# Two-batch MoE after clustered attention: order of the layers, and weights that are converted once and kept in DRAM

## Chip, cores and metric

One NeuronCore of one Trainium2 chip runs the whole program. The metric is the device time of one execution in microseconds (us); the median of three runs is given, and the profile is one profiled execution.

## What is computed

The reference runs three stages one after the other on 2 x 768 tokens:

```python
attn = softmax(where(q_assign == k_assign, q @ k.T / 8, -1e9)) @ v   # 2 batches, 8 heads, 768 x 64
x = attn as [1536, 512]                                              # 768 rows per batch
x = ((x @ w1) * (x @ w2)) @ w3 @ w_out                               # 512 -> 1024 -> 1024 -> 512
h = x @ w_in                                                         # 512 -> 2048
out = (max(h, 0) + alpha * min(h, 0)) @ w_out2                       # 2048 -> 512
```

Here q_assign and k_assign are the nearest of 16 centroids by cosine. The weights arrive as float64 and are read as pairs of 32-bit words.

## The kernel before

Every product of the MoE is made of three matmuls of split operands (mm3, L188 to L191): a float32 operand is held as a pair, hi and lo, and the product is hi x hi, hi x lo and lo x hi. On TensorE all of it is 128 x 128 weight loads, each with 384 or 512 columns streamed past.

The attention runs first, as 96 units (16 heads over both batches, 6 query tiles each), written out as a software pipeline in one loop. In the gaps of that loop (fill_steps, L606) stand the masks of later heads and, once batch 0's heads are done, the first layer of batch 0.

The MoE after it is the loop `for b in range(B)` at L731. w3 and w_out are folded into one matrix wc = w3 @ w_out, so the layers are:

- L1 (l1, L525): for each of 8 blocks f and each half a of the 768 rows, 12 matmuls for x @ w1, 12 for x @ w2, and the product of the two in PR. p_split (L725) then makes the pair ph, pl of PR: a ScalarE cast and a VectorE subtract per half.
- LC (lc, L495): the fold, 8 blocks of 24 matmuls with 512 columns. It is done once, in batch 0, after L1. Its result is kept in SBUF and also stored to DRAM (wcd) for batch 1.
- L2: x2 = PR @ wc, 4 blocks e x 2 halves x 24 matmuls, drained into the pair X2.
- L3 and L4 (l3, L777; l4, L798): 16 blocks f. l3 makes 2 x 12 matmuls with 384 columns, drained through the leaky ReLU (two ScalarE activations at L790 and L791, a VectorE combine at L792, a ScalarE cast at L795, a VectorE subtract at L796) into the pair g. l4 makes 6 x 3 matmuls with 512 columns that accumulate over all f in three PSUM tiles acc. The loop runs l3(f), then l4(f-1).

The order on TensorE is therefore L1(0), LC, L2(0), L3/L4(0), L1(1), L2(1), L3/L4(1). x_split (L509), which makes the pair of the attention's output, stands for batch 1 inside L3/L4 of batch 0.

The weights come as a stream of halves of 512 columns, in the order of the list `halves` (L69 to L80). SyncE loads a raw half (512 KB, L115), ScalarE scales its high words (w_u, L127), VectorE puts float32 words together in three instructions (w_conv, L139, L140, L143), ScalarE casts hi (L170), and GpSimd subtracts lo (L175). w_step (L157) takes the stream one half further: it emits the conversion of half n and the split of half n-1. w_goal emits a step if the stream is behind a given half, w_ready emits steps until a half is there. Both are called by hand between the matmuls, so the order on every engine is that of the code. Batch 1 loads and converts w1, w2, w_in and w_out2 a second time, and it loads wc back from DRAM. In all 120 halves are converted. There are 3 raw buffers, 4 of hi and 4 of lo, and after the attention the layers other than L4 drain through two PSUM banks (alloc_c, L722).

## Time and profile before

| | |
|---|---|
| median of 3 runs | 853.52 us (846.9, 853.52, 854.06) |
| span of the profiled execution, first to last instruction | 852.6 us |
| TensorE busy | 779.9 us, 91% |
| VectorE busy | 666.0 us, 78% |
| ScalarE busy | 508.8 us, 60% |
| GpSimd busy | 395.7 us, 46% |
| moved by DMA | 101 MB, mean 119 GB/s |

No time of the profiled execution other than its span is given; the median lies 0.9 us above the span, and that difference is carried for what lies around the span. The engines work beside each other, each in its own order. The matmuls are pipelined: the time one is shown for (0.33 us) is longer than the distance to the next start, so TensorE's pace is read from starts. Line numbers in rows of the trace are those of the kernel before.

### The profile page before, as it was taken

The page shows a single profiled execution, that of the slowest core. Times are in us where ns is not written, and L with a number is a line of the kernel's source. Part 1 is how long each engine was busy: PE and PEld are TensorE (multiplying, and loading weights), DVE is VectorE, ACT ScalarE, POOL GpSimd, SP SyncE. Part 2 cuts the span into 40 slices and gives each one's busy share as a digit, 9 for nine tenths or more (in the row PEclk, how much of TensorE's full clock was granted, in tenths as well). Part 3 has the DMA queues.
Part 4 walks back from the last instruction along what each step waited for, and adds up shares of the span by engine and source line. Part 5 has one row for each costly group of instructions (what it writes and reads, how often), then busy time and mean ns, then how long its engine had stood idle before and what let it go on. Part 6 is the DMA issues. An engine that isn't in the chain of part 4 may idle for free.

```text
span 852.6 us, 13016 instructions
## 1 busy us (share of the span) xinstructions
PE 779.9 (91%) x4497; PEld 705.1 (83%) x4497; DVE 666.0 (78%) x1020; ACT 508.8 (60%) x1092; POOL 395.7 (46%) x350
## 2 busy tenths in 40 slices
PE   5889899689999999698999989999899999999997
PEld 2778888679999989686799877888799999888886
DVE  2876899988888899969728888888666338888885
ACT  5689898777777695436434555555354335555553
POOL 0576688768485765434433343333233333333331
PEclk9799999889999999899999999999999999999999
DMA  8464333524343303536313322333432133333321
GB/s 257 146 177 142 90 94 93 145 65 117 107 126 100 107 26 125 185 124 210 117 47 108 122 101 100 123 124 122 175 124 104 49 122 122 123 107 117 124 99 75
DMA packets 35890, 101.08 MB, mean 119 GB/s; under 512 B 4496, under 2 KB 8720, under 8 KB 35824
## 3 DMA queue, kind: packets, MB, share of 16 engines
q1 hardware_dynamic: 35824, 100.25, 37.0%
q8 instruction: 36, 0.59, 0.3%
q14 instruction: 30, 0.25, 0.1%
HBM read 80.93 MB, written 5.24 MB: 101 GB/s over the span
## 4 chain that ended last, share of the span: by engine, by line
DVE 34%; PE 30%; issue 13%; ACT 8%; POOL 4%; DMA 1%; SPq 0%; POOLq 0%; DVEq 0%; ACTq 0%
DVE wt L140 13%; DVE wt L139 5%; DVE gr L792 4%; DVE wt L143 4%; ACT g L795 3%; POOL wl L175 3%; PE l L191 3%; DVE pl L465 3%; PE t L455 3%; PE l L190 3%; PE l L189 3%; PE l1b L189 2%; PE l1b L190 2%; PE l1b L191 2%; PE l1a L189 2%
## 5 line engine op out<-in xcount | busy, mean ns | idle before, releaser
L175 POOL TENSOR_TENSOR wl<-wt,wh 128x512 fp32r<-128x512 f32 x112 | 162.2, 1448 | 287.1 <-DVE g L796 171.1
L140 DVE SCALAR_TENSOR_TENSOR wt<-wr,wt 128x512 uint32<-128x512 uint32 x120 | 154.1, 1284 | 4.1
L465 DVE TENSOR_TENSOR pl<-t,ph 128x384 fp32r<-128x384 f32 x192 | 97.7, 549 | 30.7 <-ACT ph L464 30.3
L795 ACT CAST g<-gr 128x384 fp32r<-128x384 f32 x64 | 32.8, 513 | 128.5 <-DVE gr L792 128.5
L455 PE MATMUL t<-cst,p 128*128 128x128 f32 x576 | 86.6, 288 | 22.8 <-DVE pl L465 22.8
L143 DVE SCALAR_TENSOR_TENSOR wt<-wu,wt 128x512 uint32<-128x512 uint32 x120 | 102.1, 851 | 4.1
L464 ACT CAST ph<-t 128x384 fp32r<-128x384 f32 x192 | 83.5, 483 | 33.4 <-PE t L455 31.7
L191 PE MATMUL l<-x2h,wl 128*128 128x384 f32 x256 | 88.7, 347 | 11.4 <-POOL wl L175 11.4
L440 POOL TENSOR_SCALAR p<-p,su 128x768 f32<-128x768 f32 x96 | 88.3, 925 | 16.9 <-DVE su L437 14.5
L422 DVE TENSOR_REDUCE nm<-s 128x1 f32<-128x768 f32 x96 | 91.0, 947 | 4.5 <-PE s L415 4.5
L455 PEld LDWEIGHTS t<-cst,p 128*128 128x128 f32 x576 | 66.3, 146 | 32.7 <-issue 24.9
L429 ACT ACTIVATE p<-s,nm 128x768 f32<-128x768 f32 x96 | 88.0, 917 | 2.8 <-DVE nm L422 2.8
L189 PE MATMUL l<-x2h,wh 128*128 128x384 f32 x256 | 86.1, 336 | 2.2 <-ACT wh L170 2.2
L127 ACT ACTIVATE wu<-wr 128x512 f32<-128x512 f32 x120 | 81.0, 676 | 10.4 <-DMA wr<-in_w3t_dram 7.8
L190 PE MATMUL l<-x2l,wh 128*128 128x384 f32 x256 | 85.8, 335 | 0.0
L170 ACT CAST wh<-wt 128x512 fp32r<-128x512 f32 x112 | 69.3, 619 | 20.9 <-DVE wt L143 20.7
L414 PE MATMUL s<-st 128*128 128x384 f32 x192 | 76.8, 400 | 3.1 <-ACT p L429 3.1
L189 PE MATMUL acc<-wh,g 128*128 128x512 f32 x192 | 75.5, 393 | 3.5 <-ACT g L795 1.6
L476 PE MATMUL o<-ph,vs 128*128 128x256 f32 x288 | 76.8, 293 | 0.0
L191 PE MATMUL acc<-wh,g 128*128 128x512 f32 x192 | 75.9, 395 | 0.0
L190 PE MATMUL acc<-wl,g 128*128 128x512 f32 x192 | 75.7, 394 | 0.0
L477 PE MATMUL o<-pl,vs 128*128 128x256 f32 x288 | 74.9, 287 | 0.0
(132 smaller groups left out, 1907.8 us busy)
## 6 DMA issues: line engine op xcount, KB each, us to landing
wr<-in_w_dram SPq DMA_DIRECT2D x96, 512.0 KB, 3.6
wr<-in_w3t_dram SPq DMA_DIRECT2D x16, 512.0 KB, 4.3
jm<-in_qka_dram SPq DMA_DIRECT2D x12, 512.0 KB, 5.7
hr<-in_qkh_dram SPq DMA_DIRECT2D x16, 384.0 KB, 3.3
st<-st SPq DMA_DIRECT2D x16, 384.0 KB, 3.7
st<-st SPq DMA_DIRECT2D x32, 192.0 KB, 2.7
wr<-in_wo_dram SPq DMA_DIRECT2D x8, 512.0 KB, 3.2
vr<-in_vv_dram SPq DMA_DIRECT2D x8, 384.0 KB, 3.2
```

The lines of the kernel that those rows point to most:

```text
L140: nc.vector.scalar_tensor_tensor(out=t, in0=r[:, :, 0], scalar=29, in1=t, op0=ALU.logical_shift_right, op1=ALU.bitwise_or)
L143: nc.vector.scalar_tensor_tensor(out=t, in0=u, scalar=3, in1=t, op0=ALU.logical_shift_left, op1=ALU.bitwise_or)
L175: nc.gpsimd.tensor_tensor(out=lo, in0=tts.pop(n - 1), in1=f32(hi), op=ALU.subtract)
L189: nc.tensor.matmul(o, lhsT=whi, rhs=xhi, start=first, stop=False)
L190: nc.tensor.matmul(o, lhsT=whi, rhs=xlo, start=False, stop=False)
L191: nc.tensor.matmul(o, lhsT=wlo, rhs=xhi, start=False, stop=last)
L422: nc.vector.tensor_reduce(out=m, in_=scp[i][:, :, 0:HS], op=ALU.max, axis=AX.XY, negate=True)
L429: nc.scalar.activation(out=p.rearrange("p (a k) -> p a k", a=2), in_=scp.pop(i)[:, :, 0:HS], func=AF.Exp, bias=nmax.pop(i), scale=1.0, acc ...
L440: nc.gpsimd.tensor_scalar(out=pt[i], in0=pt[i], scalar1=sums[i // 2][:, i % 2 : i % 2 + 1], scalar2=1.0, op0=ALU.mult, op1=ALU.mult)
L455: nc.tensor.transpose(t[:, k], pt[i][:, kt * P : kt * P + P], ident)
L464: nc.scalar.copy(out=pth[g][:, 3 * a : 3 * a + 3, q], in_=t)
L465: nc.vector.tensor_tensor(out=ptl[g][:, 3 * a : 3 * a + 3, q], in0=t, in1=f32(pth[g][:, 3 * a : 3 * a + 3, q]), op=ALU.subtract)
```

## The change

The list of halves becomes a list `seq` with two kinds of entries. A "c" entry is a raw half that is loaded, converted and split, as before. A "k" entry loads a finished pair hi | lo (512 KB) from a DRAM tensor `kept`. Each half of w1, w2 (key "l1"), w_in and w_out2 (key "w45", second index 0 or 1) is converted once, in batch 0, and its pair is stored to `kept` from SyncE two conversions later; batch 1 has only "k" entries. The w_out2 halves of the first 10 blocks f are converted ahead of L3/L4 (key "e", stored only) and loaded back for batch 0. There are 72 conversions in place of 120, 48 stores and 58 loads of pairs. w_step is cut in two: one call emits the conversion, the next the cast and the subtract of the same half, and w_goal is called about twice as often; the loads of pairs take no call of their own. Pairs share 5 buffers of hi | lo. w_room hands on the oldest of them only when its matmuls, and its store, stand in the program. There are 4 raw buffers and 2 of converted words, in place of 3 and 3.

The order on TensorE becomes L1(0), LC block 0, then L1(1) block f and LC block f+1 in turn, then L2(0), L2(1), L3/L4(0), L3/L4(1), the last two as one loop of 33 turns. wc stays in SBUF as a pair and is split once, from PSUM, by ScalarE and VectorE. p_split of batch 0 moves in front of LC, p_split of batch 1 into L2, and x_split of batch 1 into LC's block 0. Until L3 starts, the layers drain through a ring of five PSUM tiles.

```diff
-    wcd = dp.tile([4, P, 8, P], F32, name="wcd")
-    halves = []
-    l1h = [("w", w12[f, :, k * 512 : k * 512 + 512]) for f in range(8) for k in range(2)]
-    halves += l1h[0:12] + [("wo", g) for g in range(6)] + l1h[12:16] + [("wo", g) for g in range(6, 8)]
...
+    NE = 10
+    kept = dp.tile([48, P, 2, 512], F32, name="kept")
+    seq, at, keep, need = [], {}, {}, {}
...
+    def conv(what, f, k, early=False):
+        key = (what, 0, f, k)
+        stored = what in ("l1", "w45")
+        if stored:
+            keep[what, f, k] = len(keep)
+        item("c", key, w_src(what, f, k), int(stored) + int(not early))
+    def back(what, b, f, k):
+        item("k", (what, b, f, k), keep[what, f, k], 1)
+    for f in range(6):
+        conv("l1", f, 0), conv("l1", f, 1)
+    for g in range(6):
+        conv("wo", g, 0)
+    for f in range(6, 8):
+        conv("l1", f, 0), conv("l1", f, 1)
+    for g in range(6, 8):
...
     for f in range(8):
-        halves += [("w", w3t[f, :, 0:512]), ("w", w3t[f, :, 512:1024])]
...
+        conv("w3", f, 0), conv("w3", f, 1)
+        back("l1", 1, f, 0), back("l1", 1, f, 1)
+    for f in range(NE):
+        conv("w45", f, 1, early=True)
+        at.pop(("w45", 0, f, 1))
+        need["e", f] = need.pop(("w45", 0, f, 1))
+        seq[-1] = ("c", ("e", f), seq[-1][2])
+    for f in range(16):
+        conv("w45", f, 0)
+        if f < NE:
+            back("w45", 0, f, 1)
+        else:
+            conv("w45", f, 1)
+    for f in range(16):
+        back("w45", 1, f, 0), back("w45", 1, f, 1)
+    NSEQ = len(seq)
...
+    def w_store():
+        n = stores.popleft()
+        key = seq[n][1]
+        nc.sync.dma_start(out=kept[kept_at(key)], in_=f32(whole.pop(n)))
+        w_done(key)
+    def w_room():
+        if len(held) < NWHL:
+            return True
+        while stores and need[held[0]] > 0 and seq[stores[0]][1] == held[0]:
+            w_store()
+        return need[held[0]] == 0
...
+        t = wp.tile([P, 2, 512], F32R, tag="whl", bufs=NWHL, name=f"wh{n}")
+        his[key] = t[:, 0], t[:, 1]
...
+    def w_step(force=False):
...
+        kind, key, src = seq[n]
+        if kind == "k":
+            if not w_room():
+                assert not force, key
+                return False
+            nc.sync.dma_start(out=f32(whl_tile(n)), in_=kept[src])
+            st["step"] += 1
+            return True
+        m = ordinal[n]
+        if not st["half"]:
+            w_load(m + 3)
+            while stores and ordinal[stores[0]] <= m - 2:
+                w_store()
+            w_u(m)
+            w_conv(n)
+            w_u(m + 1)
+            st["half"] = 1
+            return True
...
+        else:
+            if not w_room():
+                assert not force, key
+                return False
+            t = whl_tile(n)
+            hi, lo = his[key]
+            if key[0] in ("l1", "w45", "e"):
+                whole[n] = t
+                stores.append(n)
+        nc.scalar.copy(out=hi, in_=tts[n])
+        nc.gpsimd.tensor_tensor(out=lo, in0=tts.pop(n), in1=f32(hi), op=ALU.subtract)
+        st["half"] = 0
...
+        nc.scalar.copy(out=WO["wc"][:, 0, f], in_=t)
+        nc.vector.tensor_tensor(out=WO["wc"][:, 1, f], in0=t, in1=f32(WO["wc"][:, 0, f]), op=ALU.subtract)
...
+        def l1_steps(b, f, ahead):
+            for a in range(2):
+                if a == 0:
+                    w_ready(("l1", b, f, 1))
+                for _ in l1(b, f, a, alloc_f):
+                    w_goal(ahead)
+                    yield f
...
+        ring = deque(("c", "acc0", "c", "acc1", "acc2"))
...
+            nc.scalar.copy(out=ph, in_=PR[b][:, f, s])
+            nc.vector.tensor_tensor(out=pl, in0=PR[b][:, f, s], in1=f32(ph), op=ALU.subtract)
...
+        for f in fill:
+            w_goal(at["w3", 0, 0, 1])
+            w_goal(at["w3", 0, 0, 1])
+            if f is not None and nsp < f:
+                p_split(0, nsp, 0), p_split(0, nsp, 1)
+                nsp += 1
+        w_ready(("w3", 0, 0, 1))
+        while nsp < 8:
+            p_split(0, nsp, 0), p_split(0, nsp, 1)
+            nsp += 1
+        lc(0, alloc_c, lambda k: x_split(1, k))
+        for f in range(8):
+            nxt = min(f + 1, 7)
+            for _ in l1_steps(1, f, at["l1", 1, nxt, 1]):
+                pass
+            if f < 7:
+                w_ready(("w3", 0, f + 1, 1))
+                lc(f + 1, alloc_c, lambda k: w_goal(at["w3", 0, min(f + 2, 7), 1]))
+        X2 = {0: [st_tile(f"x2{t}").rearrange("p e s -> p e s") for t in "hl"]}
+        x = cp.tile([P, 8 * S], F32, tag="wox", name="x2_1").bitcast(F32R).rearrange("p (t e s) -> p t e s", t=2, e=4)
+        X2[1] = [x[:, 0], x[:, 1]]
+        for b, a in ((0, 0), (0, 1), (1, 0), (1, 1)):
+            s = slice(a * HS, a * HS + HS)
+            for e in range(4):
+                t = alloc_c(f"l2_{b}{e}{a}")
+                for f in range(8):
+                    if f % 4 == 0:
+                        w_goal(NSEQ)
+                    c = slice(e * P, e * P + P)
+                    wc = WO["wc"]
+                    mm3(t[:, 0:HS], wc[:, 0, f, c], wc[:, 1, f, c], PH[b, a][:, f], PL[b, a][:, f], f == 0, f == 7)
+                nc.scalar.copy(out=X2[b][0][:, e, s], in_=t[:, 0:HS])
+                nc.vector.tensor_tensor(
+                    out=X2[b][1][:, e, s], in0=t[:, 0:HS], in1=f32(X2[b][0][:, e, s]), op=ALU.subtract
+                )
+                if (b, a) == (0, 1):
+                    p_split(1, 2 * e, 0), p_split(1, 2 * e + 1, 0)
+                if (b, a) == (1, 0):
+                    p_split(1, 2 * e, 1), p_split(1, 2 * e + 1, 1)
...
+        def l3(b, f):
+            w_ready(("w45", b, f, 0))
+            hi, lo = his["w45", b, f, 0]
+            g = big(("ph0", "pl0")[f % 2], f"g{b}{f}")[:, 0 : 2 * S].bitcast(F32R).rearrange("p (t s) -> p t s", t=2)
+            w = big(("ph1", "pl1")[f % 2], f"gr{b}{f}")[:, 0 : 4 * HS].rearrange("p (a t s) -> p a t s", a=2, t=2)
+            G[b, f] = g
...
+                w_goal(NSEQ)
...
+            w_done(("w45", b, f, 0))
...
-            for f in range(17):
-                if f < 16:
-                    w_ready(n_l34(b, f))
-                    l3(f)
...
+        for i in range(33):
+            if i < 32:
+                l3(*divmod(i, 16))
+            if i > 0:
+                l4(*divmod(i - 1, 16))
```

The order of VectorE where the attention is over and the first LC block comes near (wt = words of a converted half, pr = product of L1, pl = lo part that p_split makes), before:

```order
L139 TENSOR_SCALAR wt25_4551<-wu25_4523 128x512
L140 SCALAR_TENSOR_TENSOR wt25_4551<-wr25_4505,wt25_4551 128x512
L143 SCALAR_TENSOR_TENSOR wt25_4551<-wu25_4523,wt25_4551 128x512
L139 TENSOR_SCALAR wt26_4578<-wu26_4549 128x512
L140 SCALAR_TENSOR_TENSOR wt26_4578<-wr26_4530,wt26_4578 128x512
L143 SCALAR_TENSOR_TENSOR wt26_4578<-wu26_4549,wt26_4578 128x512
L537 TENSOR_TENSOR pr0_506<-l1b070_4585,asb070_4571 128x384
```

and now:

```order
L180 SCALAR_TENSOR_TENSOR wt24_4557<-wr24_4462,wt24_4557 128x512
L183 SCALAR_TENSOR_TENSOR wt24_4557<-wu24_4533,wt24_4557 128x512
L798 TENSOR_TENSOR pl00_4472<-pr0_506,ph00_4471 128x384
L798 TENSOR_TENSOR pl01_4476<-pr0_506,ph01_4475 128x384
L179 TENSOR_SCALAR wt25_4587<-wu25_4561 128x512
L180 SCALAR_TENSOR_TENSOR wt25_4587<-wr25_4496,wt25_4587 128x512
L183 SCALAR_TENSOR_TENSOR wt25_4587<-wu25_4561,wt25_4587 128x512
```

Halves 24 and 25 are those of w3's first block, which LC block 0 reads. Before, conversions followed each other; now a pair of pl stands between them, four such pairs ahead of half 25's last instruction.

VectorE in block 4 of L3/L4 of batch 0 (gr = leaky ReLU before its split, g = its pair), before:

```order
L792 SCALAR_TENSOR_TENSOR gr040_5659<-gn040_5660,alp_71,gr040_5659 128x384
L796 TENSOR_TENSOR g04_5633<-gr040_5659,g04_5633 128x384
L139 TENSOR_SCALAR wt59_5671<-wu59_5637 128x512
L140 SCALAR_TENSOR_TENSOR wt59_5671<-wr59_5589,wt59_5671 128x512
L143 SCALAR_TENSOR_TENSOR wt59_5671<-wu59_5637,wt59_5671 128x512
L792 SCALAR_TENSOR_TENSOR gr041_5691<-gn041_5692,alp_71,gr041_5691 128x384
L796 TENSOR_TENSOR g04_5633<-gr041_5691,g04_5633 128x384
L516 TENSOR_TENSOR xs1_5523<-xr6_3489,xs1_5523 128x384
L139 TENSOR_SCALAR wt60_5726<-wu60_5669 128x512
```

and now:

```order
L183 SCALAR_TENSOR_TENSOR wt78_6444<-wu78_6378,wt78_6444 128x512
L865 SCALAR_TENSOR_TENSOR gr04_6417<-gr04_6417,alp_71 128x384
L869 TENSOR_TENSOR g04_6416<-gr04_6417,g04_6416 128x384
L865 SCALAR_TENSOR_TENSOR gr05_6487<-gr05_6487,alp_71 128x384
L869 TENSOR_TENSOR g05_6486<-gr05_6487,g05_6486 128x384
L179 TENSOR_SCALAR wt80_6514<-wu80_6448 128x512
```

Before, a conversion stood after each half of a block (and x_split's subtract in four blocks); now one stands in each block up to block 9, so that the second half of block 4 and the first half of block 5 follow each other. From the later part of block 9 to block 14 there is one after each half again, as before, and in batch 1 none.

SyncE's queue in the same blocks, before:

```order
L115 DMA wr59_5589<-in_w45_dram 128x1024
L115 DMA wr60_5644<-in_w45_dram 128x1024
L115 DMA wr61_5676<-in_w45_dram 128x1024
L115 DMA wr62_5731<-in_w45_dram 128x1024
L115 DMA wr63_5763<-in_w45_dram 128x1024
```

and now:

```order
L198 DMA wh75_6369<-kept_73 128x1024
L135 DMA wr82_6371<-in_w45_dram 128x1024
L146 DMA kept_73<-wh72_6278 128x1024
L198 DMA wh77_6439<-kept_73 128x1024
L135 DMA wr84_6441<-in_w45_dram 128x1024
```

Raw loads (wr) alone become one raw load, one store and one load of a pair per block. Pair 77 goes into the buffer of pair 72, whose store is the DMA issued just ahead of it.

## Rows read from the trace of the kernel before

**Rows 1.** Busy time by stretch; columns as the first line names them, counts in brackets
```profile
core 0: us, PE busy (x) PEld busy (x) DVE busy (x) ACT busy (x) POOL busy (x), PEclk, DMA share, GB/s
370.70:420.70 50.00, 45.73 (x193) 35.19 (x193) 43.27 (x54) 24.45 (x46) 19.00 (x14) 1.00 0.47 142
420.70:454.60 33.90, 33.60 (x193) 33.26 (x192) 14.88 (x18) 11.86 (x23) 12.37 (x9) 1.00 0.26 86
454.60:607.00 152.40, 139.68 (x674) 120.48 (x674) 127.44 (x167) 81.28 (x172) 51.60 (x36) 0.99 0.33 117
607.00:674.00 67.00, 67.00 (x386) 66.91 (x385) 40.72 (x69) 28.93 (x59) 20.75 (x16) 0.99 0.32 111
674.00:707.30 33.30, 33.30 (x194) 33.30 (x193) 13.56 (x19) 10.63 (x20) 11.38 (x9) 1.00 0.32 111
707.30:848.20 140.90, 136.46 (x673) 119.97 (x671) 115.45 (x154) 74.77 (x158) 44.08 (x30) 1.00 0.30 106
848.20:852.60 4.40, 0.14 (x1) 0.00 (x0) 0.69 (x1) 0.08 (x1) 0.00 (x0) 1.00 0.57 216
```
**Rows 2.** TensorE's timeline in one L3/L4 block: start, us, instruction, [idle before <-releaser]
```profile
468.23 0.45 PE L191 MATMUL l<-x2h,wl 128*128 128x384 f32 x1 [0.68 <-POOL wl L175]
...
470.08 0.33 PE L189 MATMUL l<-x2h,wh 128*128 128x384 f32 x1
...
472.16 0.39 PE L189 MATMUL acc<-wh,g 128*128 128x512 f32 x1
...
476.28 0.33 PE L189 MATMUL l<-x2h,wh 128*128 128x384 f32 x1
```
**Rows 3.** VectorE's timeline in the same block
```profile
466.15 0.56 DVE L796 TENSOR_TENSOR g<-gr,g 128x384 fp32r<-128x384 f32 x1 [0.58 <-ACT g L795]
466.62 0.42 DVE L139 TENSOR_SCALAR wt<-wu 128x512 uint32<-128x512 uint32 x1
467.08 1.65 DVE L140 SCALAR_TENSOR_TENSOR wt<-wr,wt 128x512 uint32<-128x512 uint32 x1
468.76 0.69 DVE L143 SCALAR_TENSOR_TENSOR wt<-wu,wt 128x512 uint32<-128x512 uint32 x1
469.37 0.61 DVE L792 SCALAR_TENSOR_TENSOR gr<-gn,alp,gr 128x384 f32<-128x384 f32 x1
470.57 0.56 DVE L796 TENSOR_TENSOR g<-gr,g 128x384 fp32r<-128x384 f32 x1 [0.58 <-ACT g L795]
```
**Rows 4.** TensorE's waits from 341 to 421 us: total us, times, longest
```profile
PE l1b L189 <- DVE pr L537: 4.6, 3, 1.6
PE lc L191 <- POOL wl L175: 4.3, 6, 0.8
PE l1a L189 <- ACT wh L170: 3.9, 1, 3.9
```
**Rows 5.** Groups by line: form, count | busy us, mean ns | idle before, releaser
```profile
L728 ACT CAST ph<-pr 128x384 fp32r<-128x384 f32 x32 | 14.8, 510 | 1.3 <-DVE pr L537 1.3
L729 DVE TENSOR_TENSOR pl<-pr,ph 128x384 fp32r<-128x384 f32 x32 | 23.2, 760 | 19.6 <-ACT ph L728 19.5
L516 POOL TENSOR_TENSOR xs<-xr,xs 128x384 fp32r<-128x384 f32 x8 | 8.1, 1012 | 12.0 <-ACT xs L515 12.0
L415 PE MATMUL s<-st 80*128 80x384 f32 x192 | 68.5, 357 | 2.1 <-DMA st<-mk 2.1
```
**Rows 6.** Two stretches of 5 us, columns as in rows 1
```profile
345.00:350.00 5.00, 4.66 (x14) 4.15 (x15) 4.86 (x6) 1.80 (x4) 2.69 (x2) 0.50 0.59 197
390.00:395.00 5.00, 4.24 (x19) 3.04 (x18) 4.93 (x6) 2.69 (x6) 2.71 (x2) 1.00 0.82 243
```
**Rows 7.** DMA issues by line: count, KB each, median us from issue to landing
```profile
wr<-in_w_dram SPq DMA_DIRECT2D x96, 512.0 KB, 3.6
wcd<-wc SPq DMA_DIRECT2D x8, 256.0 KB, 2.5
wr<-wcd SPq DMA_DIRECT2D x8, 256.0 KB, 2.5
```

More of the change, by code (lines that the diff above doesn't have):

```diff
@@ L96 @@
+    for f in range(16):
[7 more added lines that the diff above has]
+    NSEQ = len(seq)
+    raws_of = [n for n in range(NSEQ) if seq[n][0] == "c"]
+    ordinal = {n: m for m, n in enumerate(raws_of)}
     raws, his, tts, us = {}, {}, {}, {}
-    st = {"load": 0, "step": 0, "u": 0}
+    st = {"load": 0, "step": 0, "u": 0, "half": 0}
+    NWHL = 5
@@ L98 @@
     WO = {}
-    def w_load(upto):
-        while st["load"] <= min(upto, NH - 1):
-            n = st["load"]
-            kind, src = halves[n]
-            if kind == "wo":
-                src = wo[src]
-            if kind == "s":
-                st["load"] += 1
-                continue
-            r = wp.tile([P, 512, 2], U32, tag="wraw", bufs=3, name=f"wr{n}")
-            if kind == "d":
-                r = r.rearrange("p n w -> p (n w)").bitcast(F32)[:, 0:512]
-                nc.sync.dma_start(out=r, in_=src)
-            else:
-                nc.sync.dma_start(out=r.rearrange("p n w -> p (n w)"), in_=src.bitcast(U32))
+    held, whole, stores = deque(), {}, deque()
@@ L116, in w_load, with kept_at, w_done @@
+    def kept_at(key):
+        return keep[("w45", key[1], 1) if key[0] == "e" else (key[0], *key[2:])]
+    def w_load(m):
+        while st["load"] <= min(m, len(raws_of) - 1):
+            n = raws_of[st["load"]]
+            r = wp.tile([P, 512, 2], U32, tag="wraw", bufs=4, name=f"wr{n}")
+            nc.sync.dma_start(out=r.rearrange("p n w -> p (n w)"), in_=seq[n][2].bitcast(U32))
             raws[n] = r
             st["load"] += 1
-    def w_u(n):
-        if n >= NH or n != st["u"]:
+    def w_done(key):
+        need[key] -= 1
@@ new lines, in l3, with l4 @@
+                nc.scalar.copy(out=g[:, 0, s], in_=gr)
+                nc.vector.tensor_tensor(out=g[:, 1, s], in0=gr, in1=f32(g[:, 0, s]), op=ALU.subtract)
+            w_done(("w45", b, f, 0))
+        def l4(b, f):
+            w_ready(("w45", b, f, 1))
+            g = G.pop((b, f))
+            hi, lo = his["w45", b, f, 1]
+            if f == 0:
+                for j in range(3):
+                    acc[j] = pc.tile([P, 2, 512], F32, tag=f"acc{j}", name=f"acc{b}{j}")
+            if f == 15:
+                OS[b] = cp.tile([P, 8 * S], F32, tag="pr", name=f"os{b}")
+            for j in (0, 2, 4, 1, 3, 5):
+                if j < 2:
+                    w_goal(NSEQ)
+                s = slice(j * P, j * P + P)
+                mm3(acc[j // 2][:, j % 2], g[:, 0, s], g[:, 1, s], hi, lo, f == 0, f == 15)
+                if f == 15:
+                    o = OS[b][:, 512 * j : 512 * j + 512]
+                    if j in (0, 4, 3):
+                        nc.scalar.copy(out=o, in_=acc[j // 2][:, j % 2])
+                    else:
+                        nc.vector.tensor_copy(o, acc[j // 2][:, j % 2])
+                    nc.sync.dma_start(out=out[b * S + j * P : b * S + j * P + P, :], in_=o)
+            w_done(("w45", b, f, 1))
```

253 lines of the change are left out of this document (80 added, 173 removed).

## Prediction

> **What bounds the kernel now.** I read the page's busy shares first: TensorE is the busiest engine, VectorE the next. A mean says little here, so I cut the span behind the attention into its layers [rows 1]. The reader is to compare the stretches. L1 and L2 of batch 1 (607.0 to 707.3) have TensorE busy throughout. LC and both L3/L4 do not, and there VectorE is busy for 82% to 87%. How much is lost is read from TensorE's starts [rows 2]: the 12 matmuls of 384 columns from 470.08 to 472.16 start every 0.1733 us, the 18 of 512 columns from there to 476.28 every 0.2289 us. One block f of L3/L4 thus needs 24 x 0.1733 + 18 x 0.2289 = 8.28 us, 16 blocks 132.5. They took 152.4 in batch 0 (the turn of the batch included) and 140.9 in batch 1. The timelines show the cause: TensorE waits 0.68 us for GpSimd's wl at 468.23, and VectorE's cycle is 466.15 to 470.57, 4.42 us per half block, against 4.14 of TensorE [rows 2, 3]. Of the 4.42, the conversion takes 2.75 (466.62 to 469.37). LC is also paced by conversions: two halves of w3 per block of 24 x 0.2289 = 5.49 us, and p_split beside them. So after 370.7 us the matmuls alone would need 192 x 0.2289 + 768 x 0.1733 + 2 x 132.5 = 442.0 us and the tail of 4.4; the rows show 481.9. The most that the reorder can win there is 35.5 us, if nothing is added.
>
> **The change part by part.** The base is the span of 852.6; the median is 0.9 above it.
>
> LC and L1(1) in turn. Before: 50.0 + 67.0 = 117.0 [rows 1]. Now a block of LC and a block of L1 make 5.49 + 48 x 0.1733 = 13.8 us of TensorE, and VectorE has two conversions (5.5), two products (about 0.56 each, as the subtract of the same shape in rows 3) and wc's subtract (estimate from that, 0.75 for 512 columns): 7.4. The conversions hide, and 110.5 is left: **-6.5**. If this cover went, LC would be back at 50.0.
>
> L2 of both. 33.9 + 33.3 becomes 66.55, -0.65. In eight of the 16 tiles VectorE has a conversion, a drain and two subtracts of p_split, 2.75 + 0.56 + 2 x 0.56 to 0.76 = 4.4 to 4.8, against 4.16 of TensorE; the five PSUM tiles let it lag, and two or three tiles' lag can reach a p_split that the next quarter needs. From 0 to +5, taken +1: **+0.35**.
>
> L3/L4(0). Up to block 9 there is one conversion per block: 2.75 and twice the rest of the cycle (4.42 - 2.75 = 1.67) are 6.1 us, under 8.28. From there 11 conversions stand one to a half, at 4.42 for 4.14, which is 11 x 0.28 = 3.1 too much; they begin about a block and a half ahead, so I take half, 1.5, between 0 and the 9 of all 16 blocks at 8.84. The turn of the batch has L3 of the next batch between the two L4, so nothing waits there. 152.4 becomes 132.5 + 1.5: **-18.4**.
>
> L3/L4(1). No conversion is left, VectorE has 3.3 of 8.28 us, and GpSimd nothing. What can be late next is the load of a pair: 3.6 us from issue to landing [rows 7], issued when TensorE frees the buffer, about a block (8.28) ahead of its use. 140.9 becomes 132.5: **-8.4**.
>
> The way into LC. Four pairs of p_split subtracts stand among the conversions ahead of LC block 0. Each pair costs 2 x 0.56 and the wait for its first cast, 0.51 [rows 5], so 1.6, together 6.4. Against them, the 4.6 us that TensorE waited for products in two PSUM banks [rows 4] go with the ring of five: 1.8 is left. Then L1(1) needs x_split, which on ScalarE is behind all of p_split: about 0.6 to its start, seven casts of 0.51, a GpSimd subtract of 1.0 [rows 5], the last three matmuls 0.5, less 2.1 of matmuls that run meanwhile: 3.6. Sum **+5.4**. From below 0 is possible, if ScalarE and VectorE overlap better than one after the other. From above, TensorE waits some 4 us between L1(0) and LC, and after its wait of 3.9 us at 341 to 345 the granted clock was 0.50 for 345 to 350, the level of 1.2 GHz [rows 4, 6]; five such us would cost 2.5 more, and another after x_split as much: +10.5.
>
> DMA. 48 stores of 512 KB and ten extra loads for batch 0 are new; batch 1's 58 - 10 = 48 loads of pairs replace as many raw loads. In L2 a tile of 4.16 us moves a raw load and a store, 1.05 MB, 252 GB/s, and L3/L4(0) from block 10 the same. The busiest stretch shown moved 243 GB/s at a DMA share of 0.82 [rows 6], so 296 at a share of 1: it fits, with three raw loads ahead. Cost 0, up to 2. In block 4 and its like SyncE waits for a store to land before the load into the same buffer; behind it are raw loads that are three conversions ahead, so nothing waits. In the attention 12 of L1's 16 stores go past the DMAs that prepare the next heads. The whole attention waited 2.1 us for such a DMA [rows 5]. The price lies between 0 and seven heads, each late by one 512 KB transfer of 3.6 us, 25; I take the near row: **+1**.
>
> On these stores a rule of the Trainium skill speaks against the change. The rows first: 256 KB took 2.5 us to land in DRAM and 2.5 us from DRAM [rows 7], so a store costs what a load does. The Trainium skill (DMA: Bandwidth & Descriptors, section Anatomy of one DMA), of the path that GpSimd issues, says that most of a DMA's fixed time is the receipt of the write, and that this can be surprisingly long when the target is HBM. By that rule a head would be late by more than a load's time, as in the first rival; by the rows the sum stays. The trace does not agree at 256 KB, and shows no store of 512 KB.
>
> Sum: -6.5 + 0.35 - 18.4 - 8.4 + 5.4 + 1 = -26.6. Span 826.0, with the 0.9 **827.0 us**, 3.1% less.
>
> **The rivals.**
>
> Slower: the stores hold the heads. The DMAs that place a head's mask rows (st<-mk) stand behind a store in SyncE's one queue, in seven heads of the attention. For it: that order, and that TensorE is nearly full there, so what a head loses is not made up. Against it: the equal landing times of rows 7 and the 2.1 us of rows 5. Each head late by more than (26.6 + 1) / 7 = 3.9 us makes the whole slower than before. With a store at twice a load's 3.6, 7 x 7.2 = 50 us in place of my 1: 876.
>
> VectorE stays the bound. Its order is fixed by hand, so a conversion whose words come late holds the drains behind it. L3/L4(0) at 8.84 a block is 141.4, 7.4 above my 134.0; with L2's +2 more and the clock's 2.5 at the way in: 839. For it: in batch 0 the whole stage ran at VectorE's cycle [rows 3], with VectorE busy for 127.4 of 152.4 us [rows 1]. Against it: 48 of 120 conversions are gone.
>
> TensorE sets the pace everywhere: -35.5, 818. For it: 100 us of L1 and L2 without a gap [rows 1]. Against it: the way in has a chain that no other work covers.
>
> The pairs of batch 1 come no sooner than the conversions did: each load waits for TensorE to free its buffer, and SyncE takes them in order. L3/L4(1) stays at 140.9: 835. Against it: 3.6 us to land, against 8.28 of a block.
>
> **How the numbers follow.** Forecast 0.50 (its own range 820 to 834), VectorE 0.20, TensorE 0.12, late pairs 0.10, stores 0.08. The range 814 to 842 leaves out the stores, the upper end of VectorE (0.05) and a little below the TensorE case. A measurement of this kernel tells about 1% from no change, 8.5 us. Faster by over 1% is everything below 845: 0.50 + 0.12 + 0.10 + 0.17 of VectorE = 0.89. Within 1%: 0.03 of VectorE and 0.02 of the stores, heads late by some 3 us. Slower: 0.06 of the stores.
>
> **What would show it.** LC and L1(1) together should take 110 to 117 us with their starts 0.1733 and 0.2289 apart; both L3/L4 some 134 and 132.5, without a wait of TensorE for wl in the second; a wait of TensorE of 3 to 4 us ahead of LC and again ahead of L1(1); stores that land in about 3.6 us. Wrong would be: LC's first matmul later than about 374 us with waits for st<-mk in the attention (the stores), a cycle of 4.4 us per half block in L3/L4(0) (VectorE), or waits of TensorE for a DMA of pairs (late pairs).

## The result, and the profile after

The changed kernel takes 830.78 us (median of 4, 829.38 to 831.89), the kernel before 852.57 beside it: a ratio of 0.974, with a 95% interval of 0.970 to 0.978. The prediction was 827.0. The profiled execution of the changed kernel has a span of 829.6 us; against the 826.0 predicted for it the miss is 3.6 us. That small miss hides two large ones of opposite sign: that they nearly cancel is luck, as the table below shows.

First the stretches, cut as in [rows 1] (columns as there). L1(0) ends just ahead of the first; then come LC and L1(1) in turn, L2 of both batches, L3/L4(0), L3/L4(1) and the tail. The cut between the last two is the first matmul of batch 1's L3, so one L4 of batch 0 (18 x 0.2289 = 4.1 us) stands in the second of them. From here on, line numbers in rows are those of the kernel that the row comes from.

```profile
366.20:486.70 120.50, 117.59 (x577) 106.31 (x578) 58.04 (x84) 38.23 (x75) 26.30 (x20) 0.95 0.40 139
486.70:555.90 69.20, 67.38 (x385) 66.49 (x384) 41.21 (x71) 27.96 (x56) 16.78 (x13) 1.00 0.62 190
555.90:687.30 131.40, 130.22 (x657) 117.28 (x656) 75.59 (x121) 62.80 (x133) 25.41 (x19) 1.00 0.57 180
687.30:825.20 137.90, 137.34 (x691) 123.92 (x689) 42.15 (x71) 47.23 (x103) 0.00 (x0) 1.00 0.42 138
825.20:829.60 4.40, 0.18 (x1) 0.00 (x0) 0.69 (x1) 0.13 (x1) 0.00 (x0) 0.88 0.58 218
```

TensorE is busy for over 99% of both L3/L4 stretches now, against 92% and 97% in [rows 1], and VectorE for 31% in batch 1. LC and L1(1) took 120.5 us, not 110.5. Where the 10 us went is read from TensorE's waits between 341 and 400 us (total, times, longest) and from two stretches of 5 us.

```profile
PE l1a L242 <- ACT wh L224: 4.2, 1, 4.2
PE lc L242 <- ACT wh L224: 3.9, 1, 3.9
PE l1a L242 <- ACT xs L569: 2.1, 1, 2.1
PE l1a L244 <- POOL wh L225: 0.9, 1, 0.9
PE l1a L243 <- POOL xs L570: 0.6, 1, 0.6
```

```profile
365.00:370.00 5.00, 3.67 (x8) 2.47 (x9) 3.83 (x6) 2.39 (x5) 1.29 (x1) 0.50 0.78 272
...
380.00:385.00 5.00, 5.00 (x15) 4.08 (x15) 4.54 (x6) 1.65 (x4) 1.80 (x2) 0.52 0.02 4
```

The wait of 3.9 us ends at 366.18, and LC 0 then runs at a granted clock of 0.50, the 1.2 GHz level. After the waits for xs (2.1 and 0.6) L1(1)'s first block runs at 0.52. No wait for a conversion is left after 400 us. TensorE's timeline shows the starts of LC's block 1, of L1(1)'s block 1 and of LC's block 2:

```profile
389.88 0.39 PE L242 MATMUL lc<-wo,wh 128*128 128x512 f32 x1
...
395.36 0.33 PE L242 MATMUL l1a<-xs,wh 128*128 128x384 f32 x1
...
403.71 0.39 PE L242 MATMUL lc<-wo,wh 128*128 128x512 f32 x1
```

A block of LC takes 5.5 us there and one of L1 8.4. LC's block 0 took 8.7 (366.18 to 376.94 less the wait of 2.1), L1(1)'s block 0 12.3 (from there to 389.88 less the wait of 0.6). So some 7 of the 10 us went with the lower clock behind the two waits, and 2.7 with the waits of L1(1) themselves.

The term by term account, in us (span of before 852.6, of after 829.6):

| term | predicted | measured | how it is read |
|---|---|---|---|
| attention | +1 | -4.8 | its last matmul of s starts at 306.7, before at 311.5 (in the other runs below at 305.3 to 307.5) |
| way into LC | +5.4 | +10.3 | LC's first matmul 366.2 against 370.7 is -4.5, of which -4.8 is the attention: +0.3; and 120.5 - 110.5 = 10.0 behind it |
| LC and L1(1) in turn, apart from that | -6.5 | -6.5 | 117.0 to 110.5, the matmuls' own time; from LC's block 1 at 389.9 to L2 at 486.7 seven blocks of each took 96.8, and need 7 x 13.8 = 96.7 |
| L2 | +0.35 | +2.0 | 67.2 to 69.2 |
| L3/L4, both | -26.8 | -24.0 | 293.3 to 131.4 + 137.9 = 269.3 |
| sum | -26.6 | -23.0 | |

The DMA issues of the changed kernel (count, KB each, median us from issue to landing):

```profile
wh<-kept SPq DMA_DIRECT2D x58, 512.0 KB, 3.3
wr<-in_w_dram SPq DMA_DIRECT2D x48, 512.0 KB, 4.5
kept<-wh SPq DMA_DIRECT2D x48, 512.0 KB, 5.4
```

A store of 512 KB takes 5.4 us to land, a load of the same pair 3.3. So the equal times at 256 KB of [rows 7] do not carry over, and the 3.6 us that the prediction named for a store was too short. The Trainium skill (DMA: Bandwidth & Descriptors, section Anatomy of one DMA) says, of the path that GpSimd issues, that most of a DMA's fixed time is the receipt of the write, and that this can be surprisingly long when the target is HBM. The trace of these stores, which SyncE issues, agrees in the direction (5.4 against 3.3); how much of it is the receipt it does not show, since raw loads of 512 KB took 4.5. What this costs is another question, answered by run e5.

### The profile page after: what moved, and what is told of

Its sections match the earlier page's. It is cut to its first block, busy times and chain, and to the rows that moved or that the text cites. A ratio compares the mean times of both kernels' runs of the same rounds, so it can differ in the third digit from the quotient of the medians.

```text
span 829.6 us, 12623 instructions
## 1 busy us (share of the span) xinstructions
PE 771.8 (93%) x4497; PEld 707.8 (85%) x4497; DVE 523.2 (63%) x884; ACT 452.4 (55%) x980; POOL 300.6 (36%) x286
## 5 line engine op out<-in xcount | busy, mean ns | idle before, releaser
L225 POOL TENSOR_TENSOR wh<-wt,wh 128x512 fp32r<-128x512 f32 x64 | 85.5, 1336 | 264.3 <-ACT wh L224 176.0
L865 DVE SCALAR_TENSOR_TENSOR gr<-gr,alp 128x384 f32<-128x384 f32 x64 | 41.6, 651 | 107.4 <-ACT gr L864 107.4
L493 POOL TENSOR_SCALAR p<-p,su 128x768 f32<-128x768 f32 x96 | 91.4, 958 | 17.4 <-DVE su L490 14.9
L224 ACT CAST wh<-wt 128x512 fp32r<-128x512 f32 x64 | 39.7, 621 | 77.9 <-issue 53.1
L863 ACT ACTIVATE gr<-l 128x384 f32<-128x384 f32 x64 | 31.2, 487 | 81.1 <-PE l L244 81.1
L244 PE MATMUL acc<-wh,g 128*128 128x512 f32 x192 | 75.3, 392 | 0.0
L242 PE MATMUL acc<-wh,g 128*128 128x512 f32 x192 | 74.8, 390 | 0.6 <-ACT os L889 0.6
L243 PE MATMUL acc<-wh,g 128*128 128x512 f32 x192 | 75.3, 392 | 0.0
L468 PE MATMUL s<-st 80*128 80x384 f32 x192 | 68.4, 356 | 2.4 <-DMA st<-mk 2.4
L183 DVE SCALAR_TENSOR_TENSOR wt<-wu,wt 128x512 uint32<-128x512 uint32 x72 | 67.6, 938 | 2.5
L180 DVE SCALAR_TENSOR_TENSOR wt<-wr,wt 128x512 uint32<-128x512 uint32 x72 | 59.1, 821 | 2.5
L869 DVE TENSOR_TENSOR g<-gr,g 128x384 fp32r<-128x384 f32 x64 | 35.7, 558 | 37.1 <-ACT g L868 37.1
```

The source lines that it names most:

```text
L225: nc.gpsimd.tensor_tensor(out=lo, in0=tts.pop(n), in1=f32(hi), op=ALU.subtract)
L242: nc.tensor.matmul(o, lhsT=whi, rhs=xhi, start=first, stop=False)
L243: nc.tensor.matmul(o, lhsT=whi, rhs=xlo, start=False, stop=False)
L244: nc.tensor.matmul(o, lhsT=wlo, rhs=xhi, start=False, stop=last)
L493: nc.gpsimd.tensor_scalar(out=pt[i], in0=pt[i], scalar1=sums[i // 2][:, i % 2 : i % 2 + 1], scalar2=1.0, op0=ALU.mult, op1=ALU.mult)
```

## The experiments

Each run is compared with the changed kernel's 830.8 us, runs e10 to e12 also with each other. The kernel before ran again beside each group of runs, with medians from 851.2 to 853.0; so of two runs that were not timed side by side, a difference of 2 us shows nothing by itself.

**Attention: the pace of the first conversions (e1).** The table's largest surprise is 4.8 us gained in a part that the prediction thought untouched. VectorE's maxima (nm, 96 of them, one per unit) serve as a clock of the attention. The 49th and the 64th, first in the kernel before, then in the changed one (start, us, instruction):

```profile
155.64 0.95 DVE L422 TENSOR_REDUCE nm<-s 128x1 f32<-128x768 f32 x1
...
212.17 0.95 DVE L422 TENSOR_REDUCE nm<-s 128x1 f32<-128x768 f32 x1
```

```profile
154.98 0.95 DVE L475 TENSOR_REDUCE nm<-s 128x1 f32<-128x768 f32 x1
...
207.52 0.95 DVE L475 TENSOR_REDUCE nm<-s 128x1 f32<-128x768 f32 x1
```

15 units take 56.5 us before and 52.5 after; up to there, and from there to the attention's end, the two drift apart by no more than 1 us. In this stretch the first conversions of L1 stand. Before, three came in three calls in a row; in the new step a call does either the conversion or the split, so the same calls hold two. Run e1 puts three in a row back:

```diff
-            for _ in range(4):
-                w_goal(1)
+            for k in range(4):
+                if k < 3:
+                    w_goal(k)
+                    w_goal(k)
                 yield
```

> The changed kernel with the first three conversions of L1's pairs in three units of the attention in a row again (both halves of a step, the conversion and the split, in one unit), as before the change; nothing else is moved. Theory A, the attention ended 4.7 us earlier after the change because its first conversions now come in every second unit: L1(0)'s first matmul goes from 185.4 to about 189 us, two waits of TensorE for pl near 165 instead of one, the whole 3 to 4.5 us slower, about 834.5. Theory B, those 4.7 us are chance of one execution: 829 to 832.5, L1(0)'s first matmul at 185 to 186.

Measured: 836.07 us (833.67 to 837.01), 5.3 slower. The same two maxima in e1:

```profile
151.75 0.95 DVE L475 TENSOR_REDUCE nm<-s 128x1 f32<-128x768 f32 x1
...
207.94 0.95 DVE L475 TENSOR_REDUCE nm<-s 128x1 f32<-128x768 f32 x1
```

56.2 us: in these 15 units the loss is back. In the other profiled executions with the new pace (the changed kernel, e2 to e12) they take 52.2 to 54.3, so theory A has the place right: the pace of the first conversions costs 2 to 4 us there. The rest of A did not come. This execution was 3.2 us ahead at the 49th maximum, L1(0) began at 187.6, not 189, TensorE waited for xt as well as for pl, and the attention's last matmul of s starts at 306.8, as in the changed kernel (306.7). LC's first matmul starts at 366.2 in both, so the 2.3 us by which this span is longer (831.9) lie behind it. That the first conversions make the 5.3 us of the whole is therefore not shown.

**Do the stores hold the heads? (e5)**

```diff
-        nc.sync.dma_start(out=kept[kept_at(key)], in_=f32(whole.pop(n)))
+        for c in (1, 0):
+            nc.sync.dma_start(out=kept[c, kept_at(key)], in_=f32(whole[n]))
+        whole.pop(n)
```

(kept has a first dimension of 2, and loads read its first half.)

> Each of the 48 stores of a pair is issued twice (into two places in DRAM), 24 MB more. Theory A, stores hold no head, since SyncE's queue and the DMA engines have room: the wait of the attention for st<-mk stays near 2.4 us, L1(0)'s first matmul and the end of the attention within 1 us, the whole 830 to 833. Theory B, a store delays the DMAs of the next head by its landing time (5.4 us), hidden in one execution by the attention's gain elsewhere: the attention 10 to 35 us longer with waits for st<-mk of some us per head, the whole 840 to 866.

Measured: 831.28 us (830.26 to 833.68). The store's row and, from the waits of the attention, the wait for st<-mk:

```profile
kept<-wh SPq DMA_DIRECT2D x96, 512.0 KB, 6.5
```

```profile
PE s L470 <- DMA st<-mk: 2.9, 2, 2.4
```

Twice the stores, each landing later still, cost 0.5 us, which is within what the runs scatter. L2 moved 274 GB/s there and L3/L4(0) 255, without a longer stage. The rival is right in part: mask rows that SyncE issues right behind a store do land later. In e5, first two mask rows behind a pair of stores (issued from 186.6 us), then two with no store just ahead (from 207.7):

```profile
DMA to landing us min/median/max: 4.7/5.2/5.7
...
DMA to landing us min/median/max: 2.3/2.5/2.7
```

From the issue of the stores to the landing of the second row it is 6.9 to 7.4 us in the three heads that this meets in e5, 5.8 to 6.3 in the changed kernel, and some 3 us from the first row's issue where no store stands just ahead. But TensorE takes these rows up only later. Both waits for st<-mk above lie before 150 us, and the first store is issued at 186. The head with the least to spare had its rows 2.2 us before the weight load that reads them in the changed kernel (landed at 274.2, read at 276.4), and 1.1 us in e5 (273.9 and 275.0). So the rival with 7.2 us per head falls: a head's rows are some 3 us late, 4 when the stores are doubled, and this is hidden.

**The way into LC (e2, e3, e4, e6).** VectorE's timeline in the changed kernel, ahead of LC, shows the cycle of one pair of p_split and one conversion; below it ScalarE's.

```profile
351.72 1.01 DVE L798 TENSOR_TENSOR pl<-pr,ph 128x384 fp32r<-128x384 f32 x2
...
356.72 1.81 DVE L798 TENSOR_TENSOR pl<-pr,ph 128x384 fp32r<-128x384 f32 x2 [1.10 <-ACT ph L797]
358.45 0.41 DVE L179 TENSOR_SCALAR wt<-wu 128x512 uint32<-128x512 uint32 x1
358.90 0.69 DVE L180 SCALAR_TENSOR_TENSOR wt<-wr,wt 128x512 uint32<-128x512 uint32 x1
359.63 0.69 DVE L183 SCALAR_TENSOR_TENSOR wt<-wu,wt 128x512 uint32<-128x512 uint32 x1
361.42 1.34 DVE L798 TENSOR_TENSOR pl<-pr,ph 128x384 fp32r<-128x384 f32 x1 [1.10 <-ACT ph L797]
```

```profile
360.35 0.62 ACT L224 CAST wo<-wt 128x512 fp32r<-128x512 f32 x1 [2.30 <-DVE wt L183]
360.88 0.92 ACT L797 CAST ph<-pr 128x384 fp32r<-128x384 f32 x2
```

The cycle is 361.42 - 356.72 = 4.70 us. The cast of ph stands behind the cast of the weight, which waits for the end of VectorE's conversion; so VectorE idles 1.10 us and then does the two subtracts in 1.81, while GpSimd subtracts too (alone they take 1.0). Such a pair costs 2.9 us, not the 1.6 of the prediction; the first one, at 351.72, cost 1.0. e2 moves all pairs behind the conversions that LC 0 needs:

```diff
         for f in fill:
             w_goal(at["w3", 0, 0, 1])
             w_goal(at["w3", 0, 0, 1])
-            if f is not None and nsp < f:
-                p_split(0, nsp, 0), p_split(0, nsp, 1)
-                nsp += 1
```

> All eight pairs of p_split(0) behind the last conversion that LC 0 needs, instead of one pair after each two steps. Theory A, a pair among conversions costs VectorE 2.9 us (1.10 idle for a cast that stands behind the cast of wh on ScalarE, 1.8 for two subtracts beside GpSimd), a pair behind them 1.1: LC's first matmul at about 362.5 without a wait of 4 us, x_split at about 370, L1(1) from about 371.5 with a wait of some 4 us ahead of it; the whole 3 to 6 us faster, about 826. Theory B, the way into LC is VectorE's fixed sum of work, in whatever order: LC starts 4 us earlier, L1(1) at 376 to 378 as now, the whole within 1.5 us of 830.8.

Measured: 827.86 us (826.64 to 829.21), 2.9 faster, half way between the theories. LC starts at 362.9 without a wait of 4 us, as A said. But behind it TensorE waits for xs twice, as its timeline shows:

```profile
372.64 0.69 PE L242 MATMUL l1a<-xs,wh 128*128 128x384 f32 x1 [3.37 <-ACT xs L569]
376.32 0.69 PE L243 MATMUL l1a<-xs,wh 128*128 128x384 f32 x1 [2.99 <-POOL xs L570]
```

The second wait was not foreseen: GpSimd's subtracts of x_split begin at 372.67 beside VectorE's row of p_split subtracts, which ends at 374.0, and all four take 7.44 us, where they took 4.84 in the changed kernel.

e3 keeps four pairs there and puts x_split ahead of the other four:

```diff
-            if f is not None and nsp < f:
+            if f is not None and nsp < min(f, 4):
...
+        lc(0, alloc_c, lambda k: x_split(1, k))
         while nsp < 8:
             p_split(0, nsp, 0), p_split(0, nsp, 1)
             nsp += 1
-        lc(0, alloc_c, lambda k: x_split(1, k))
```

> Four pairs of p_split(0) stay among the conversions, x_split of batch 1 comes ahead of the other four. Theory A, the order of x_split behind all pairs costs the second wait (2.1 + 0.6 us) and the half clock after it (some 5 us), and the last four pairs hide behind L1(1)'s first block in the ring of five PSUM tiles: no wait of over 1 us ahead of L1(1), the whole 6 to 10 us faster, about 822. Theory B, the four pairs hold back the first product of L1(1), the ring fills, and the wait goes there: 826 to 830.

Measured: 827.70 us (826.92 to 828.08), 3.1 faster. A's sign holds and its size does not; the time lies in B's range: ahead of L1(1) only 0.5 us is left to wait, but LC still waits 2.7 us and then 1.4 more, in four waits, for its words. L2 begins at 481.2 instead of 486.7, 5.5 earlier; in this execution L2 gave 1.6 of that back (below, under the clock).

e4 changes what stands first: L1(1) needs no conversion, so blocks 0 to 2 of it go ahead of LC 0 (the loop is one block further than the run's expectation says), x_split ahead of the last three pairs and wholly on VectorE.

```diff
+    NA = 2
...
+    for f in range(NA):
+        back("l1", 1, f, 0), back("l1", 1, f, 1)
...
+        x_split(1)
         while nsp < 8:
...
-        lc(0, alloc_c, lambda k: x_split(1, k))
-        for f in range(8):
...
+        for f in range(8 + NA):
+            if f < 8:
+                for _ in l1_steps(1, f, at["w3", 0, max(f + 1 - NA, 0), 1]):
+                    pass
+            if f >= NA:
+                w_ready(("w3", 0, f - NA, 1))
+                lc(f - NA, alloc_c, lambda k: w_goal(at["w3", 0, min(f + 2 - NA, 7), 1]))
```

> Two blocks of L1(1), which need no conversion, stand ahead of LC 0, so the order is L1(1) 0, 1, LC 0, L1(1) 2, LC 1 and so on, with LC 6 and 7 after each other at the end; x_split of batch 1 comes ahead of the last three pairs of p_split(0), its first half first, all on VectorE. Theory A, the way in costs what VectorE does between L1(0) and L1(1), and conversions for LC have cover once two blocks of L1 stand ahead: a wait of 1.3 to 2 us between L1(0) and L1(1), no other over 1 us, LC + L1(1) in 111 to 113 us, the whole 10 to 13 us faster, about 819. Theory B, VectorE's debt only moves: TensorE waits about 4 us for wh at LC 0, and again before LC 7, 826 to 830.

Measured: 824.29 us (822.60 to 824.80), 6.5 faster, which is between the theories. No wait for wh at LC 0, so B's debt did not come back. Left are 1.2 us between L1(0) and L1(1), 1.8 behind it, and a granted clock of 0.69 from 365 to 370; LC and L1(1) take 364.3 to 479.7 = 115.4 us.

e6 gives the ring up:

```diff
-        ring = deque(("c", "acc0", "c", "acc1", "acc2"))
+        ring = deque()
```

> The ring of five PSUM tiles is two tiles again for L1(0)'s end, LC, L1(1) and L2. Theory A, the ring takes away the 4.6 us that L1(0) waited for products before the change, and lets VectorE lag in L2: the whole 4 to 9 us slower, 835 to 840, with waits of TensorE for pr in L1. Theory B, L1(0)'s end goes by VectorE's conversions either way, and the wait for products only takes time that would else be waited for wh: 829 to 833.

Measured: 831.30 us (828.73 to 833.07), 0.5 slower: B. TensorE waits 7.1 us for products in L1(0), LC starts at 376.7 instead of 366.2, and by then x_split is done: the waits for LC's words and for xs are gone. Here the ring only moves the wait. The 4.6 us that the prediction credited to it did come (L1(0) ended some 3.7 us earlier than the attention explains) and were spent in the 3.9 us ahead of LC.

**Conversions in L3/L4 (e7, e9).** e7 converts batch 1's words again, in the new order (`again("w45", f, 0), again("w45", f, 1)` in place of the two `back`; the pairs are still stored).

> L3/L4 of batch 1 converts its 32 halves again from the raw words instead of loading the kept pairs; the order is the new one. Theory A, without kept pairs VectorE's cycle of 4.42 us per half block sets the pace: L3/L4(1) goes from 137.9 to some 145 us with waits of TensorE for wh, the whole 7 to 10 us slower, about 839. Theory B, the four raw buffers and five pairs of the new kernel are what smooths the stage, whichever way the pairs come: L3/L4(1) within 2 us of 137.9, the whole 830 to 833.

Measured: 857.65 us (855.89 to 861.32), 26.9 slower, and slower than the kernel before (ratio 1.007, 1.004 to 1.009). Right was the sign alone. From batch 1's first L3 to the end it is 168.1 us against 142.3. TensorE's waits in that stage, and VectorE's timeline:

```profile
PE acc L245 <- ACT os L892: 8.5, 1, 8.5
PE l L245 <- ACT gr L867: 8.1, 21, 0.5
```

```profile
724.19 0.42 DVE L182 TENSOR_SCALAR wt<-wu 128x512 uint32<-128x512 uint32 x1
...
732.00 0.99 DVE L868 SCALAR_TENSOR_TENSOR gr<-gr,alp 128x384 f32<-128x384 f32 x1 [1.51 <-ACT gr L867]
...
734.05 0.42 DVE L182 TENSOR_SCALAR wt<-wu 128x512 uint32<-128x512 uint32 x1
```

A block takes 734.05 - 724.19 = 9.86 us, not the 8.84 that twice the 4.42 of [rows 3] gives: in the new order VectorE also waits 1.51 us per block for ScalarE's gr. At the turn of the batch the wait of 8.5 us (acc<-os) comes on top. So the new order of L3/L4 alone would have lost, and the kept pairs carry the gain.

e9 takes away the halves converted early (`NE = 0`).

> NE = 0: no half of w_out2 is converted ahead in L2 and read back; batch 0's L3/L4 has two conversions in each of its 16 blocks. Theory A, with two conversions per block the new order of L3/L4 runs at the 9.85 us per block that run e7 showed: 16 x 1.57 = 25 us over TensorE's 8.28, less what the five pairs hold ahead, so L3/L4(0) some 20 us longer, L2 about 2 shorter, the whole 845 to 852. Theory B, two conversions cost what the prediction took, 8.84 us per block: L3/L4(0) some 8 us longer, the whole 836 to 840.

Measured: 838.57 us (836.78 to 838.90), 7.8 slower. L3/L4(0) takes 552.7 to 694.7 = 142.0 us (10.6 more), L2 66.5 (2.7 less). The total is B's; the rate is A's, as VectorE's timeline shows, and below it TensorE's waits in the stage:

```profile
599.63 0.42 DVE L179 TENSOR_SCALAR wt<-wu 128x512 uint32<-128x512 uint32 x1
...
609.46 0.42 DVE L179 TENSOR_SCALAR wt<-wu 128x512 uint32<-128x512 uint32 x1
```

```profile
PE l L242 <- ACT gr L864: 6.4, 17, 0.5
```

A block takes 609.46 - 599.63 = 9.83 us. A lead would reconcile the two: with the five pairs held, two and a half blocks, it is 13.5 x 9.83 + 8.28 = 141.0. That the lead is this long was worked out, not varied.

**A version that beats both (e8, e10, e11, e12).** TensorE's wait of 4.2 us for wh inside L1(0) (the list from 341 to 400 us) has another cause: six conversions of w_out stand ahead of those of L1's block 6. e8 adds to e4 a new order of seq; it also puts three instead of five pairs ahead of x_split, each between a conversion and its split:

```diff
     for f in range(6):
         conv("l1", f, 0), conv("l1", f, 1)
-    for g in range(6):
+    for g in range(3):
         conv("wo", g, 0)
-    for f in range(6, 8):
-        conv("l1", f, 0), conv("l1", f, 1)
-    for g in range(6, 8):
+    conv("l1", 6, 0), conv("l1", 6, 1)
+    for g in range(3, 5):
+        conv("wo", g, 0)
+    conv("l1", 7, 0), conv("l1", 7, 1)
+    for f in range(2):
+        back("l1", 1, f, 0), back("l1", 1, f, 1)
+    for g in range(5, 8):
         conv("wo", g, 0)
```

> Run e4's order, and three things more: the conversions of w_out for blocks 3 to 7 stand behind those of L1's blocks 6 and 7 (the last three behind the loads of L1(1) 0 and 1), three instead of five pairs of p_split(0) stand ahead of x_split, and each stands between a conversion and its split. Theory A, the waits left in e4 come from conversions of w_out ahead of L1's (4.2 + 0.9 us at 338 to 345 and the half clock to 350) and from pairs ahead of x_split (1.8 us and the half clock to 371): both go, L1(0) and L1(1) run without a wait of over 1.5 us, the whole 8 to 11 us faster than e4's 824.3, about 815. Theory B, the conversions moved come back as a wait at LC 0, or VectorE is late for L1's 6 and 7 anyway: 820 to 825.

Measured: 824.62 us (823.33 to 827.52), no better than e4, as B had it. But the first part went as A said: no wait for wh in L1(0) (2.3 us for a product are left), 0.6 us between L1(0) and L1(1), which starts at 359.1 instead of e4's 364.3. Then TensorE lost it again (TensorE's timeline of e8; below it SyncE's issues):

```profile
383.72 0.66 PE L248 MATMUL l1a<-xs,wh 128*128 128x384 f32 x1 [7.30 <-DVE wt L186]
```

```profile
372.02 6.91 SPq L141 DMA_DIRECT2D wr<-in_w3t_dram  x3
379.02 0.86 SPq L204 DMA_DIRECT2D wh<-kept  x2
```

The loads of the kept pairs for block 2 need nothing but a free buffer, but stand in the one queue behind raw loads, and these wait for VectorE to free theirs. VectorE's wt is only the end of that chain. e10 moves these two loads up, and those of every later block by one place:

```diff
-    for g in range(5, 8):
-        conv("wo", g, 0)
+    conv("wo", 5, 0), conv("wo", 6, 0)
+    back("l1", 1, 2, 0), back("l1", 1, 2, 1)
+    conv("wo", 7, 0)
```

> Run e8 with the loads of the pairs of L1(1) block 2 put ahead of the last conversion of w_out and of those for LC 0, instead of behind them (later blocks one place earlier too). Theory A, the wait of 7.3 us that took e8's gain back is a load of a kept pair that stands in SyncE's one queue behind raw loads, which wait for VectorE to free their buffers: it goes, with the half clock behind it, and the whole is 8 to 10 us faster than e8's 824.6, about 815. Theory B, VectorE's conversions for LC 0 are late anyway, and the wait comes back there as a wait for wh: 820 to 825.

Measured: 815.04 us (812.98 to 816.93), 9.6 faster than e8: A. The loads are issued 9 us earlier, and LC and L1(1) take 111.4 us, 0.9 over what the matmuls need (SyncE's issues of e10, then its stretch):

```profile
369.89 1.69 SPq L205 DMA_DIRECT2D wh<-kept  x2
```

```profile
359.00:470.40 111.40, 110.91 (x577) 102.88 (x578) 66.89 (x99) 40.51 (x79) 25.38 (x19) 1.00 0.47 161
```

e11 and e12 are e10 with `NE = 13` and `NE = 16`.

> Run e10 with 13 instead of 10 halves of w_out2 converted ahead in L2 (six loads of kept pairs and stores are not more, only earlier). Theory A, the last six blocks of L3/L4(0), with two conversions each at 9.8 us, take the 1.2 us of waits for gr; with three such blocks none is left, the whole 1 to 2 us faster, about 813.5. Theory B, TensorE's waits there are covered by the five pairs held, and three conversions more in L2 make VectorE late for p_split: L2 longer by 1 to 3 us, the whole 815 to 818.

> Run e10 with all 16 halves converted ahead in L2, each block of L3/L4(0) with one conversion. Theory A: no wait for gr, L3/L4(0) at TensorE's pace, L2 within 1 us of e10's 69.5, the whole 1 to 2 us faster, about 813.5. Theory B: the 16 conversions fill L2 (32 steps for 32 half conversions), the lead into L3/L4(0) is gone and VectorE late for p_split: L2 2 to 5 us longer, the whole 816 to 820.

Measured: e11 812.01 us (811.27 to 812.91), e12 820.79 (820.01 to 821.44). In e11 L3/L4(0) takes 128.7 us where e10 has 131.3, and no wait for gr is left; L2 is the same: A. In e12 L2 is not longer either, against B, but the lead is gone, as B had it: TensorE waits at the first L3 (the waits of e12 from 538 to 560 us),

```profile
PE l L249 <- ACT wh L231: 5.0, 2, 4.5
PE l L251 <- POOL wh L232: 1.2, 2, 0.7
```

and runs on at a granted clock of 0.50 from 544 to 549. e11 is the fastest version: a ratio of 0.954 to the kernel before (0.952 to 0.956), 18.8 us below the changed kernel. Between e11 and e10 (0.956, 0.953 to 0.959) these ratios do not decide; the stage does.

## Why the prediction was right or wrong

The forecast's mechanism was right: TensorE's pace where the conversions go, and a price at the way in. That the total came within 3.6 us is luck. Without the attention's gain, which nothing in the prediction foresaw (5.8 us against its term), the span would have been 835.4. The steps behave so:

- **LC and L1(1) in turn**: -6.5 was right for everything behind the entry; e10 shows the whole in 111.4 us once the entry is free.
- **L3/L4**: -26.8 predicted, -24.0 measured. The kept pairs do it (e7), and batch 1 waits for nothing but 0.6 us at the turn. About half of the missing 2.8 us is batch 0's VectorE overrun: the stage took 131.4 us, 3.0 over its matmuls (16 L3, 15 L4: 128.4), where 1.5 was charged. The cycle with two conversions is 4.92 us per half block in the new order, not the 4.42 taken from the old, while the lead that reconciles e9 is two and a half blocks, not one and a half; the two errors partly cancel. e11, with three such blocks less, gains 2.6 us in the stage. The other half is batch 1 at 137.9 us against 136.6 (16 L3, 17 L4), with the wait of 0.6 in it; the rest of it was not broken down.
- **L2**: +0.35 against +2.0. TensorE waited 1.2 us for ph and 0.5 for pl at the next quarter: the lag that I took at 1.0 of a possible 5. With no early conversion (e9) the stage takes 66.5, the matmuls' own time.
- **Way into LC**: +5.4 against +10.3, at its upper bound of 10.5, and not by the terms that were added up. The waits came in lower than charged: LC's start +0.3 for +1.8, x_split 2.7 for 3.6. The wait ahead of LC (3 to 4 us predicted, 3.9 measured) was seen rightly. The term that was mis-sized is the clock, put at 0 in the value and at 2.5 for each wait in the range: it took some 7 us behind the two waits. "Each pair costs 1.6" was wrong too: the first cost 1.0 and the next ones 2.9 each, since I priced them by operations of the old neighbourhood, where no cast of a weight stood ahead of them on ScalarE. But only three pairs stand ahead of the words that LC waited for, 6.8 us where 6.4 was charged for four, so that error hardly shows in the sum.
- **Attention**: +1 against -4.8. I looked at the added stores and not at the conversions, though the order of VectorE's rows was there to read. Run e1 shows the pace of the first conversions as the cause in 15 units (2 to 4 us); the rest is not explained. The stores cost nothing that can be measured (e5).
- **DMA**: cost 0, right, up to twice the stores.

Of the rivals, the stores are refuted by e5, and late pairs did not occur in the changed kernel, but did in L1(1) of e8 (7.3 us), by half of the chain named: SyncE takes its transfers in order. What the queue stood for was VectorE, not TensorE. VectorE stays a bound only at the way in, at one turn in L2 and for the last six blocks of L3/L4(0). TensorE's pace everywhere behind LC's old start at 370.7 us would be a span of 817.1; e11, with the attention's and L1(0)'s gains besides, has 810.4.

What stays open: how much of e1's 5.3 us is the attention. The profile shows 3.6 in the 15 units, and none at the attention's end; this execution was the fastest of its four, and no slower one was profiled. And how much of the -4.8 is the pace: the kernel before was profiled once, and the first 48 units alone scatter by some 3 us between executions.

## What to carry to other kernels

Price a moved step in its new neighbourhood: what stands ahead of it on each engine's queue decides (a 1.0 us pair became 2.9, an independent load inherited 7.3). Price a wait of TensorE with the clock behind it: behind L1(1)'s waits of 2.7 us the lower clock took another 4. Where a chain of small operations stands at a turn between stages, put the work that needs none of it first and let the chain run behind it. When a helper that serves several stages changes its step, look at every stage that calls it, also at the one that the change was not about.
